# Attention and channel mix on one core: two 64-key score blocks merged into 64 columns before the softmax

## The chip, the cores and the metric

The kernel runs on one core of a Trainium2 chip. The metric is device time in microseconds (us). The engines are PE (TensorE, matrix products and transposes), DVE (VectorE), ACT (ScalarE), POOL (GpSimd) and SP (SyncE, which here issues all DMAs). Every engine runs its own list of instructions strictly in order; semaphores hold an instruction until what it reads has been made. SBUF is the on-chip memory that all engines read, PSUM the accumulator memory that PE writes (8 banks of 128 partitions x 512 float32).

## The reference

Window attention, then a channel mix in the manner of RWKV, all in float32 (the weights arrive as float64, eight bytes each):

```
q, k, v: (8 batches, 8 heads, 576, 64)            # window 64
scores = (q @ k^T) / 8;  key j counts for query i if 0 <= i - j < 64, else -1e9
attn   = exp(scores - rowmax);  attn /= (rowsum + 1e-9);  x = attn @ v     -> (8, 576, 512)
x_prev = x shifted by one position, zero at the start of each batch
xk = mu_k * x + (1 - mu_k) * x_prev               # mu_r the same for xr
xr = mu_r * x + (1 - mu_r) * x_prev
k  = relu(xk @ w_k)          # w_k 512 x 1024
v  = (k * k) @ w_v           # w_v 1024 x 512
r  = sigmoid(xr @ w_r)       # w_r 512 x 512
out = r * v
```

A query sees at most 64 keys. Cut into blocks of 64 positions, query row r of a block sees keys r+1 to 63 of the block before and keys 0 to r of its own.

## The kernel before

**Attention.** The 8 x 9 blocks of 64 queries are taken for two heads at a time (a head pair fills 128 partitions). A group holds up to 8 such halves; there are 37 groups. For each group PE makes the scores, 128 key columns for each query, in two PSUM banks `s` (one for each head of the pair). DVE runs 8 fused instructions (scale, add the mask, negate, running minimum) over 128 columns each, from `s` to the SBUF tile `pr`; ACT makes 8 exponentials with row sums; DVE adds the epsilon and takes reciprocals (`rs`); POOL scales 8 pieces of `pr` by `rs`; PE transposes them in two blocks of four (`t`, one bank); ACT copies the two banks to `pt`; PE multiplies by the values (`x`, 128 keys deep, one bank) and ACT copies the result to `xT`, one row of 576 positions for each channel chunk and batch.

**Mix.** The 72 blocks are then taken in 11 units of 4, 5 and nine times 7 blocks, so 256, 320 or 448 columns. For each unit and each of 4 channel chunks, `d = x - x_prev` is made and blended with mu, once for xk and once for xr (in the first two units ACT makes mu-scaled x_prev instead of the difference). Each float32 operand of the products is split into a high and a low part, and every product is three matmul passes; a unit has 240 matmuls into the PSUM banks `m`, of which there are four. ACT makes the high parts, POOL or DVE the low ones.

**Weights.** 20 chunks of 128 x 512 float64 (4 of w_r, 8 of w_k, 8 of w_v) are loaded and turned into float32 by bit operations: ACT takes an absolute value, DVE clamps (in SBUF), shifts into a PSUM bank `wp` (one of the `m` banks), merges the sign and exponent there and merges the low word back into SBUF (`wt`); ACT and POOL then split high and low (`ws`).

**What sets the order.** All this is written as pieces with an engine, a key, a cost, needs and the buffers that they take. `play()` steps through time: on each engine that is free it starts the piece with the lowest key whose needs are done (plus a lag) and whose buffers are free. The engines' lists in the compiled program follow that order. An initial load gets a lag from a running count of bytes (`bus`); a load with a key (a prefetch of a later group) gets a fixed lag. `BEGIN` gives the keys of the attention groups, `DECODE` those of the weight chunks; the mix of unit u has keys from 40 u. In the profile the helper's line (74 before) stands for nearly all instructions, so tiles are told apart by name.

The pieces that the change touches are `soften` (softmax of a group), `scores` and `values`, `keep_x`, `decode`, `mix`, `transfer` and the loads.

Of the kernel before, what the change touches and what calls it, by code (L numbers as in the profile page):

```python
# [14 lines left out]
ALU = mybir.AluOpType  # L15
PSUM = bass.MemoryType.PSUM
# [7 lines left out]
G = 4  # L24
UNITS = (4, 5) + (7,) * 9
TU = max(UNITS) * W
# [3 lines left out]
FAR = 3.0e38  # L30
# [3 lines left out]
XB = 9  # L34
TB = 5
# [9 lines left out]
EARLY = 7  # L45
# [7 lines left out]
def attn_rwkv_kernel(ctx, tc, qT, kT, v2, mu_k, mu_r, w_k, w_v, w_r, out):  # L53
# [6 lines left out]
    ps_s = ctx.enter_context(tc.tile_pool(name="ps_s", bufs=2, space=PSUM))  # L60
    ps_t = ctx.enter_context(tc.tile_pool(name="ps_t", bufs=1, space=PSUM))
    ps_x = ctx.enter_context(tc.tile_pool(name="ps_x", bufs=1, space=PSUM))
    ps_m = ctx.enter_context(tc.tile_pool(name="ps_m", bufs=4, space=PSUM))


    class Engine:
# [5 lines left out]
        def __getattr__(self, name):  # L72
# [4 lines left out]
    room = {"tmp": TB, "m": 4, "s": 2, "t": 1, "x": 1, "pr": 3, "sums": 4, "pt": 2, "xT": XB,  # L77
            "ks": 8, "r": R_BUFS, "xr": 1, "xk": 1, "qk": 2, "v": 3}
# [59 lines left out]
    def over(n):  # L138

        return 75 + 1.15 * n  # L140


# [5 lines left out]
    masks = {}  # L148
    for first in (None, 0, 1):
        masks[first] = const.tile([P, P], F32, name=f"mask{first}")  # L150
        nc.gpsimd.memset(masks[first], 0.0)
        for j in range(2):
            m = masks[first][j * W:(j + 1) * W]
            if j == first:
                nc.gpsimd.affine_select(out=m, in_=m, compare_op=ALU.is_ge, fill=NEG, base=0,
                                        pattern=[[-1, P]], channel_multiplier=1)
                continue
            nc.gpsimd.affine_select(out=m, in_=m, compare_op=ALU.is_ge, fill=NEG, base=-1,
                                    pattern=[[1, P]], channel_multiplier=-1)
            nc.gpsimd.affine_select(out=m, in_=m, compare_op=ALU.is_ge, fill=NEG, base=W,  # L160
                                    pattern=[[-1, P]], channel_multiplier=1)
# [5 lines left out]

# [19 lines left out]

    words = {}

    def decode(n, loaded):
        ws, _, i, c = chunks[n]
        key = DECODE[n]
        word, bits = Hold("tmp"), Hold("m")
# [5 lines left out]
        def clamp():  # L202
# [8 lines left out]
        def top():  # L211
            dve.scalar_tensor_tensor(words[n, 0], raw[n][:, :, 1], 0xC0000000, words[n, 0],
                                     op0=ALU.bitwise_and, op1=ALU.bitwise_or)

        def low():
            dve.scalar_tensor_tensor(words[n].bitcast(U32), raw[n][:, :, 0], 29, words[n, 0],
                                     op0=ALU.logical_shift_right, op1=ALU.bitwise_or)
# [8 lines left out]
        p = Piece("ACT", key, 680, sign, [loaded], takes=[word])  # L226
        p = Piece("DVE", key, 440, clamp, [p])
        p = Piece("DVE", key, 725, shift, [p], takes=[bits])
        p = Piece("DVE", key, 725, top, [p])
        p = Piece("DVE", key, 725, low, [p], uses=[bits])  # L230
        p0 = Piece("ACT", key, 630, first_part, [p])
# [14 lines left out]
    def load_qk(n, i0=0, i1=NB, key=None):  # L246

        takes = []
        if i0 == 0:
            held[n] = [Hold("xT"), Hold("xT")] if n in (2, 3) else [Hold("qk")]  # L250
            takes = held[n]

        def load():
            if i0 == 0:
                places(n)
            q, k = loaded[n]
            dma.dma_start(k[:, i0 * W:i1 * W], kT[n, :, i0 * W:i1 * W])
            dma.dma_start(q[:, i0 * W:i1 * W], qT[n, :, i0 * W:i1 * W])

        p = transfer(load, 2 * 4 * P * W * (i1 - i0), takes, key=key)  # L260
        arrived.update(((n, i), p) for i in range(i0, i1))

    def places(n):

        if n in (2, 3):
            loaded[n] = [act.tile([P, 1 + S], F32, name=nm, tag="xT", bufs=XB)[:, :S] for nm in "qk"]
        else:
            loaded[n] = [ld.tile([P, S], F32, name=nm) for nm in "qk"]

    def load_v(n, c0=0, c1=4, d0=0, d1=4, key=None):  # L270

        takes = []
        if c0 == 0:
            held["v", n] = [Hold("ks"), Hold("ks")] if n == 3 else [Hold("v")]
            takes = held["v", n]

        def load():
            if c0 == 0:
                if n == 3:
                    v = [act.tile([P, 4, P], F32, name="vs", tag="ks", bufs=8) for _ in range(2)]  # L280
                else:
                    v = ld.tile([P, 2, 4, P], F32, name="v", bufs=3)
                    v = [v[:, 0], v[:, 1]]
                loaded["v", n] = v
            v = loaded["v", n]
            dma.dma_start(v[0][:, c0:c1], v2[n, :, 0, c0:c1])
            dma.dma_start(v[1][:, d0:d1], v2[n, :, 1, d0:d1])

        p = transfer(load, 4 * P * P * (c1 - c0 + d1 - d0), takes, key=key)
        arrived.update(((n, 0, c), p) for c in range(c0, c1))  # L290
        arrived.update(((n, 1, c), p) for c in range(d0, d1))


    def slot(*blocks):
        return list(zip(blocks[::2], blocks[1::2]))

    groups = [slot(*((n, i) for n in (n0, n0 + 1) for i in range(i0, i0 + 4)))
              for i0 in (0, 4) for n0 in (0, 2)] + [slot(*((n, NB - 1) for n in range(NP)))]
    blocks = [(n, i) for n in range(NP, B * NP) for i in range(NB)]
    groups += [slot(*blocks[o:o + 2 * G]) for o in range(0, len(blocks), 2 * G)]  # L300

    first = {n: min(t for t, sl in enumerate(groups) for s in sl for m, _ in s if m == n)
             for n in range(B * NP)}
    banks, weights, sums, flipped = {}, {}, {}, {}
    xTs, got = {}, {}
    chain = {}

    def new_xT():

        xT = act.tile([P, 1 + S], F32, name="xT", tag="xT", bufs=XB)  # L310
        dve.memset(xT[:, 0:1], 0.0)
        return xT

    def chunk(i):
        return (0, i // 2) if (i % 2 or i == 0) else (1, i // 2 - 1)

    def scores(t):

        banks[t] = [ps_s.tile([P, G, P], F32, name="s") for _ in range(2)]
        for e, halves in enumerate(groups[t]):  # L320
            for j, (n, i) in enumerate(halves):
                q, k = loaded[n]
                k0 = max(i - 1, 0) * W
                for h in range(2):
                    hr = slice(h * W, (h + 1) * W)
                    pe.matmul(banks[t][h][j * W:(j + 1) * W, e, :], q[hr, i * W:(i + 1) * W],
                              k[hr, k0:k0 + P], start=True, stop=True)

    def values(t):
        ps = flipped[t] = ps_x.tile([P, 2 * G, W], F32, name="x")  # L330
        for o, (n, i, e, j) in enumerate(order(t)):
            a, c = chunk(i)
            for h in range(2):
                pe.matmul(ps[h * W:(h + 1) * W, o, :], loaded["v", n][a][:, c, h * W:(h + 1) * W],
                          flipped[t, h][:, e, j * W:(j + 1) * W], start=True, stop=True)

    def order(t):
        return sorted((n, i, e, j) for e, halves in enumerate(groups[t]) for j, (n, i) in enumerate(halves))

    def burst(t, ts, tv):  # L340

        needs, takes, uses, cost = [], [], [], 400
        if ts is not None:
            for n, i in (half for halves in groups[ts] for half in halves):
# [362 lines left out]
```

## Time and profile before

| What | Value |
|---|---|
| Median of 3 runs | 677.83 us (677.21 to 679.62) |
| Span of the profiled execution | 676.3 us |
| PE busy | 641.3 us (95%) |
| DVE busy | 422.9 us (63%) |
| ACT busy | 373.1 us (55%) |
| POOL busy | 346.8 us (51%) |
| Moved by DMA | 56.50 MB, 84 GB/s over the span |

The profile is one execution and has no time of its own beside the span; the median of the runs lies 1.5 us above it. Busy times of PE are modelled from pipelined starts, so a row's mean is the latency of one matmul, and starts that follow each other give its cost. A row of the timeline is: start, length, engine, line, operation, output<-input tiles, shape, count. The mean busy share hides that the program has two stages, a start in which weights come in and are decoded, and a long stretch in which they stay in SBUF.

### The profile page before, as it was taken

The numbers are of one execution on the slowest core, as the hardware profiler recorded it, in microseconds if no ns is written. First come the engines' busy times: TensorE is split into PE (matmuls) and PEld (weight loads), VectorE is DVE, ScalarE is ACT, GpSimd is POOL, SyncE is SP. The second block draws the span as 40 slices with busy tenths as digits, with TensorE's granted clock in tenths as the row PEclk, the third lists the DMA queues.
The fourth block names the chain that finished last, engine by engine and source line by source line (L and its number), as shares of the span: only waits on it lengthen the run. The fifth ranks groups of instructions, "written<-read, shape, count | busy, mean of one in ns | idle before, by whom it ended". The sixth has DMA issues, their size and how long they took to land.

```text
span 676.3 us, 14360 instructions
## 1 busy us (share of the span) xinstructions
PE 641.3 (95%) x5232; PEld 575.0 (85%) x5232; DVE 422.9 (63%) x1358; ACT 373.1 (55%) x1127; POOL 346.8 (51%) x503
## 2 busy tenths in 40 slices
PE   4749799999999999999999999999999999999997
PEld 3538689998888888888898789888888888999997
DVE  5899964844882696367648615952794397276241
ACT  6878777656763765665465526535654662242330
POOL 5756785584455555455554625454563465244310
PEclk9868899999999999999999999999999999999999
DMA  8971324222321224312212202232213000001001
GB/s 258 329 301 61 105 75 127 78 97 67 109 83 63 68 70 143 108 67 81 74 36 68 95 28 67 67 108 80 67 64 122 6 1 28 29 1 38 17 1 55
DMA packets 33766, 56.50 MB, mean 84 GB/s; under 512 B 5024, under 2 KB 16800, under 8 KB 33696
## 3 DMA queue, kind: packets, MB, share of 16 engines
q1 hardware_dynamic: 33696, 55.59, 24.3%
q8 instruction: 41, 0.67, 0.4%
q14 instruction: 29, 0.24, 0.1%
HBM read 46.14 MB, written 9.44 MB: 82 GB/s over the span
## 4 chain that ended last, share of the span: by engine, by line
PE 79%; DVE 9%; POOL 5%; issue 3%; ACT 2%; DMA 1%; SPq 0%; POOLq 0%; ACTq 0%
PE m L74 64%; PE x L74 5%; PE s L74 5%; PE t L74 4%; DVE d L74 3%; POOL pr L74 3%; DVE r L74 2%; DVE ks L74 1%; POOL ws L74 1%; DMA q<-qT 1%; DVE pr L74 1%; DVE wt L74 1%; DVE wp L74 1%; DVE th L74 1%; ACT pr L74 1%
## 5 line engine op out<-in xcount | busy, mean ns | idle before, releaser
L74 PE MATMUL m<-xk,ws 128*128 128x448 f32 (+2 forms) x1056 | 221.1, 359 | 0.0
L74 PE MATMUL m<-ks,ws 128*128 128x448 f32 (+2 forms) x1056 | 218.1, 356 | 2.2 <-DVE ks L74 2.2
L74 PEld LDWEIGHTS m<-ks,ws 128*128 128x128 f32 x1056 | 186.6, 188 | 16.3 <-DVE ks L74 2.6
L74 PEld LDWEIGHTS m<-xk,ws 128*128 128x128 f32 x1056 | 188.2, 191 | 13.6
L74 POOL TENSOR_SCALAR pr<-pr,rs 128x128 f32<-128x128 f32 x288 | 133.7, 482 | 114.2 <-DVE rs L74 97.7
L74 DVE TENSOR_TENSOR ks<-kf,ks 128x448 fp32r<-128x448 f32 (+2 forms) x88 | 60.7, 702 | 123.1 <-ACT ks L74 122.5
L74 POOL TENSOR_TENSOR kf<-kf 128x448 f32<-128x448 f32 (+2 forms) x88 | 79.3, 905 | 108.8 <-ACT kf L74 108.4
L74 PE MATMUL m<-xr,ws 128*128 128x448 f32 (+2 forms) x528 | 113.3, 359 | 8.3 <-ACT r L74 5.6
L74 ACT ACTIVATE pr<-pr,nmax 128x128 f32<-128x128 f32 x288 | 111.9, 393 | 10.7 <-DVE nmax L74 8.1
L74 PEld LDWEIGHTS m<-xr,ws 128*128 128x128 f32 x528 | 94.6, 191 | 16.3 <-ACT r L74 5.8
L74 ACT COPY pt<-t 128x512 f32<-128x512 f32 (+1 forms) x74 | 42.4, 574 | 74.3 <-PE t L74 74.1
L74 POOL TENSOR_TENSOR xk<-d,xk 128x448 fp32r<-128x448 f32 (+2 forms) x44 | 55.3, 1263 | 39.4 <-ACT xk L74 39.4
L74 DVE TENSOR_TENSOR d<-xT 128x448 f32<-128x448 f32 (+6 forms) x120 | 72.1, 604 | 0.2
L74 ACT ACTIVATE kf<-m 128x448 f32<-128x448 f32 (+2 forms) x88 | 44.8, 516 | 45.3 <-PE m L74 42.2
L74 PE MATMUL t<-ident,pr 128*128 128x128 f32 x288 | 51.9, 289 | 13.7 <-POOL pr L74 11.1
L74 ACT CAST ks<-kf 128x448 fp32r<-128x448 f32 (+2 forms) x88 | 46.4, 543 | 29.6 <-POOL kf L74 29.6
L74 POOL TENSOR_TENSOR xr<-d,xr 128x448 fp32r<-128x448 f32 (+2 forms) x44 | 50.6, 1164 | 22.7 <-ACT xr L74 22.7
L74 DVE CUSTOM_DVE_ANT_0 pr<-s,maskNone 128x128 f32<-128x128 f32 x224 | 53.8, 285 | 12.1 <-PE s L74 12.0
L74 DVE SCALAR_TENSOR_TENSOR r<-m,r 128x448 f32<-128x448 f32 (+2 forms) x44 | 25.8, 591 | 55.3 <-PE m L74 55.3
L74 PEld LDWEIGHTS t<-ident,pr 128*128 128x128 f32 x288 | 37.2, 144 | 26.6 <-POOL pr L74 20.2
L74 ACT ACTIVATION_READ_ACCUMULATOR pr<-pr,nmax 128x1 f32 x288 | 54.9, 191 | 0.0
L74 PE MATMUL s<-k,q 64*64 64x128 f32 x1152 | 44.5, 294 | 7.0 <-DMA q<-qT 6.9
(46 smaller groups left out, 578.8 us busy)
## 6 DMA issues: line engine op xcount, KB each, us to landing
v<-v SPq DMA_DIRECT2D x56, 256.0 KB, 4.1
k<-kT SPq DMA_DIRECT2D x28, 288.0 KB, 2.8
q<-qT SPq DMA_DIRECT2D x28, 288.0 KB, 3.3
w<-w_k SPq DMA_DIRECT2D x8, 512.0 KB, 6.3
w<-w_v SPq DMA_DIRECT2D x8, 512.0 KB, 10.2
outT<-r SPq DMA_DIRECT2D x12, 224.0 KB, 1.9
w<-w_r SPq DMA_DIRECT2D x4, 512.0 KB, 4.5
outT<-r SPq DMA_DIRECT2D x12, 160.0 KB, 1.8
```

The lines of the kernel that those rows point to most:

```text
L74: return lambda *args, **kw: tc.keep_in_program_order(op(*args, **kw))
```

## The change

One change in many places:

- **Groups** are now 36 pairs of blocks with all 8 heads each. Each group loads its own q (128 x 4 x 128), k (128 x 4 x 192) and v (six tiles of 64 rows, one for each half of the partitions and each of three blocks).
- **Scores** are the same matmuls, into one tile `s` of two banks. `pack` then merges the two key blocks: where a mask `own` (key column not after the query row) is set, a predicated copy puts the score of the query's own block over that of the block before, in PSUM; 512 columns remain for 8 heads x 2 blocks. A reduction takes the maximum, one subtraction writes `pr`.
- **Softmax** on those 512 columns: one exponential on ACT, `shares` (a sum, the epsilon, a reciprocal) on DVE, one multiplication by the reciprocals on POOL.
- **Transposes**: four for each group (144 in all, 288 before). `keep` copies the bank twice, on DVE, each time multiplied by a mask of one side (`sides`), into `pt`.
- **Values**: 64 matmuls of 64 keys x 64 columns for each group, own block and previous block accumulated, into two banks `x`.
- **x** lies in `xu`, one tile for each unit with all 4 chunks. In `mix` the difference `d` is made once and used for xk and xr.
- **Decode** is in place in SBUF: the four DVE instructions are one piece and take no PSUM bank.
- PSUM: `s` one tile of two banks, `t` one, `x` two, `m` three. The `spare` rule goes, costs and `BEGIN` are new, the fixed lag of a keyed load is 2600 instead of 2000.

```diff
-BEGIN = (-30, -29, 0, 6, 12, 18, 26, 34, 43, *range(53, 184, 10),
+BEGIN = (-30, -28, 2, 14, 24, 34, 43, *range(53, 184, 10),
          196, 210, 223, 236, 250, 263, 277, 286, 295, 304, 312, 322, 332, 342, 352)
...
-    room = {"tmp": TB, "m": 4, "s": 2, "t": 1, "x": 1, "pr": 3, "sums": 4, "pt": 2, "xT": XB,
-            "ks": 8, "r": R_BUFS, "xr": 1, "xk": 1, "qk": 2, "v": 3}
+    room = {"tmp": TB, "m": 3, "s": 1, "t": 1, "x": 1, "pr": 2, "sums": 4, "pt": 2, "xu": 2,
+            "ks": 8, "r": R_BUFS, "xr": 1, "xk": 1, "q": 2, "k": 2, "v": 3}
...
-        def shift():
-            words[n, 0] = ps_m.tile([P, WC], U32, name="wp", tag="m")
-            dve.tensor_scalar(words[n, 0], words[n].bitcast(U32), 3, 0x3FFFFFF8,
-                              op0=ALU.logical_shift_left, op1=ALU.bitwise_and)
...
+        def bits():
+            word = words[n].bitcast(U32)
+            dve.tensor_scalar(words[n], words[n], HI_MIN, HI_MAX, op0=ALU.max, op1=ALU.min)
+            dve.tensor_scalar(word, word, 3, 0x3FFFFFF8, op0=ALU.logical_shift_left, op1=ALU.bitwise_and)
+            dve.scalar_tensor_tensor(word, raw[n][:, :, 1], 0xC0000000, word, op0=ALU.bitwise_and, op1=ALU.bitwise_or)
+            dve.scalar_tensor_tensor(word, raw[n][:, :, 0], 29, word, op0=ALU.logical_shift_right, op1=ALU.bitwise_or)
...
-        p = Piece("SP", len(pieces) - 9999 if key is None else key, 60, fn, needs, takes, lag=2000)
+        p = Piece("SP", len(pieces) - 9999 if key is None else key, 60, fn, needs, takes, lag=2600)
...
+        def pack():
+            s8 = s4.rearrange("q h e k -> q (h e) k")
+            if block(g, 0)[1] and block(g, 1)[1]:
+                dve.copy_predicated(s8[:, :, :W], wide(own.bitcast(U32), 8), s8[:, :, W:])
...
+            dve.tensor_reduce(sums[g][0], s8[:, :, :W], axis=AX.X, op=ALU.max)
+            dve.tensor_sub(weights[g], s8[:, :, :W], sums[g][0].unsqueeze(2).to_broadcast([P, 8, W]))
+        def exp():
+            sca.activation(weights[g], weights[g], AF.Exp, scale=SCALE)
+        def shares():
+            dve.tensor_reduce(total, weights[g], axis=AX.X, op=ALU.add)
+            dve.tensor_scalar_add(rs, total, EPS)
+            dve.reciprocal(rs, rs)
+        def scale():
+            pool.tensor_mul(weights[g], weights[g], sums[g][2].unsqueeze(2).to_broadcast([P, 8, W]))
+        def flip():
+            for e in range(4):
+                pe.transpose(ps[:, e], weights[g][:, 2 * e:2 * e + 2].rearrange("q e k -> q (e k)"), ident)
+        def keep():
+            for a in (1, 0):
+                dve.tensor_mul(sided[g][:, a].rearrange("q e (j r) -> q (e j) r", j=2),
+                               flipped[g].rearrange("q e (j r) -> q (e j) r", j=2), wide(sides[:, a], 8))
...
+    def prefetch(t):
+        for what, g in (("q", t + 2), ("k", t + 2), ("v", t + 2)):
+            if 2 <= g < GROUPS:
+                load(what, g, key=BEGIN[t])
...
+    load("q", 0)
+    load("k", 0)
+    load_w(2)
+    load("v", 0)
+    load("q", 1)
+    load("k", 1)
+    load_w(2)
+    load("v", 1)
+    load_w(len(chunks) - len(raw))
```

The order of instructions changes most at the start. On SP, before, the first rows are the loads of q and k of the first head pairs among the first weight chunks (`q_128`, `k_129` and so on are those of one head pair):

```order
L74 DMA w_126<-w_r 128x1024
L74 DMA k_129<-kT 128x256
L74 DMA q_128<-qT 128x256
L74 DMA k_133<-kT 128x256
L74 DMA q_132<-qT 128x256
L74 DMA w_136<-w_r 128x1024
L74 DMA k_139<-kT 128x256
L74 DMA q_138<-qT 128x256
L74 DMA k_143<-kT 128x256 [waits DMAHW0_49]
```

In the changed kernel SP holds at these places (`q_108`, `k_112` and `q_123`, `k_125` belong to groups 0 and 1, `q_196`, `k_208` to group 2):

```order
L71 DMA q_108<-qT 128x4x128
L71 DMA k_112<-kT 128x4x128
...
L71 DMA q_123<-qT 128x4x128 [waits DMAHW0_49]
L71 DMA k_125<-kT 128x4x192 [waits DMAHW1_49]
...
L71 DMA w_168<-w_v 128x1024 [waits DMAHW2_49]
L71 DMA w_170<-w_v 128x1024 [waits DMAHW3_49]
...
L71 DMA q_196<-qT 128x4x128 [waits DMAHW2_49,PE_49]
L71 DMA k_208<-kT 128x4x192 [waits DMAHW3_49]
```

The eight semaphores DMAHW0 to DMAHW7 are taken in turn, so `q_196` is issued once the transfer of `w_168` has landed, and `k_208` once that of `w_170`, the last weight chunk, has. Both stood nowhere near this place before: no load of the first four groups was behind the last weight chunks.

On PE, before, two groups of scores come first, then transposes and values of the first group:

```order
L74 MATMUL s<-k,q 64x128 [waits DMAHW2_49,DMAHW1_49]
L74 MATMUL s<-k,q 64x128 x7
L74 MATMUL s<-k,q 64x128 [waits DMAHW4_49,DMAHW3_49]
L74 MATMUL s<-k,q 64x128 x7
L74 MATMUL s<-k,q 64x128 [waits DMAHW6_49,DMAHW7_49,DVE_49,PE_49]
L74 MATMUL s<-k,q 64x128 [waits DVE_49,PE_49]
L74 MATMUL s<-k,q 64x128 x6
L74 MATMUL s<-k,q 64x128 [waits DMAHW1_49,DMAHW0_49]
L74 MATMUL s<-k,q 64x128 x7
L74 MATMUL t<-ident,pr 128x128 [waits Pool_49] x4
```

Now (`s_179` is group 0, `s_219` group 2, `s_274` group 1, `t_262` and `x_300` group 0):

```order
L71 MATMUL s_179<-k_112,q_108 64x64 [waits DMAHW1_49,DMAHW0_49]
L71 MATMUL s_179<-k_112,q_108 64x64 x7
L71 MATMUL s_179<-k_112,q_108 64x128 x8
L71 MATMUL s_219<-k_208,q_196 64x128 [waits DMAHW2_49,DMAHW3_49,DVE_49,PE_49]
L71 MATMUL s_219<-k_208,q_196 64x128 x15
L71 MATMUL t_262<-ident_82,pr_198 128x128 [waits Pool_49]
L71 MATMUL t_262<-ident_82,pr_198 128x128 x3
L71 MATMUL s_274<-k_125,q_123 64x128 [waits DMAHW0_49,DMAHW1_49,DVE_49,PE_49]
L71 MATMUL s_274<-k_125,q_123 64x128 x15
L71 MATMUL x_300<-pt_270,v_118 64x64 [waits DMAHW4_49,DVE_49]
```

The scores of group 2 now stand as the second burst of all, ahead of the transposes of group 0 and the scores of group 1.

DVE follows with the decode chunks behind that burst's first reader. Before, its list begins with the first chunk and the maxima of group 0:

```order
L74 TENSOR_SCALAR wt<-wt 128x512 [waits Activation_49]
L74 TENSOR_SCALAR wp<-wt 128x512 [waits DVE_49]
L74 SCALAR_TENSOR_TENSOR wp<-w,wp 128x512 [waits DMAHW0_49,DVE_49]
L74 SCALAR_TENSOR_TENSOR wt<-w,wp 128x512 [waits DVE_49]
L74 ISA pr,nmax<-s,mask_101 128x128 [waits PE_49,Pool_49]
```

Now, after the pack of group 0, two chunks and the mu vectors (`wt_268` is the third chunk):

```order
L71 TENSOR_SCALAR mu1_107<-muk_105 128x4 [waits DMAHW2_49]
L71 TENSOR_SCALAR mu1_107<-mur_106 128x4 [waits DMAHW3_49]
L71 COPY_PREDICATED s_219<-own_87,s_219 128x8x64 [waits PE_49]
L71 TENSOR_REDUCE most_256<-s_219 128x8 [waits DVE_49]
L71 TENSOR_TENSOR pr_255<-s_219,most_256 128x512 [waits DVE_49]
L71 TENSOR_TENSOR pt_270<-t_262,sides_89 128x512 [waits PE_49,Pool_49]
L71 TENSOR_TENSOR pt_270<-t_262,sides_89 128x512
L71 TENSOR_SCALAR wt_268<-wt_268 128x512 [waits Activation_49]
```

The predicated copy of `s_219` reads the scores of group 2. The decode of `wt_268`, the third chunk, and of the seventeen after it stand behind that row in DVE's list.

More of the change, by code (lines that the diff above doesn't have):

```diff
@@ L224, in second_part @@
             pool.tensor_sub(ws[i, c][:, 1], words[n], ws[i, c][:, 0].bitcast(F32))
[L226 to L231, printed above, removed]
+        p = Piece("ACT", key, 600, sign, [loaded], takes=[word])
+        p = Piece("DVE", key, 2000, bits, [p])
+        p0 = Piece("ACT", key, 540, first_part, [p])
         decoded[id(ws), i, c] = p0, Piece("POOL", key, 1280, second_part, [p0], uses=[word])
@@ L329, in values @@
[L329 to L338, printed above, removed]
@@ new lines, in block, with scores @@
+    def block(g, s):
+        return divmod(2 * g + s, NB)
+    banks, weights, sums, flipped, sided, crossed = {}, {}, {}, {}, {}, {}
+    xs_of, got, opened_x = {}, {}, {}
+    chain = {}
+    def scores(g):
+        banks[g] = ps_s.tile([P, 2, 4, P], F32, name="s")
+        q, k = loaded["q", g], loaded["k", g]
+        for s in range(2):
+            o = 0 if block(g, s)[1] else W
+            for p in range(2):
+                for h in range(2):
+                    for j in range(2):
+                        hr, n = slice(h * W, (h + 1) * W), 2 * j + p
+                        pe.matmul(banks[g][j * W:(j + 1) * W, h, 2 * s + p, o:], q[hr, n, s * W:(s + 1) * W],
+                                  k[hr, n, s * W + o:(s + 2) * W], start=True, stop=True)
@@ L356, in burst @@
+    def burst(key, gs, gv):
+        needs, takes, uses, cost = [], [], [], 100
+        if gs is not None:
+            needs += [arrived["q", gs], arrived["k", gs]]
+            uses += [held["q", gs], held["k", gs]]
+            takes.append(Hold("s"))
+            cost += 900
+        if gv is not None:
             bank = Hold("x")
+            needs += [arrived["v", gv], chain["kept", gv]]
+            uses += [held["v", gv], chain["pt", gv]]
             takes.append(bank)
+            cost += 1050
@@ L359, in fn @@
         def fn():
-            if ts is not None:
-                scores(ts)
-            if tv is not None:
-                values(tv)
-        p = Piece("PE", BEGIN[t] if t < len(BEGIN) else BEGIN[-1] + 9, cost, fn, needs, takes, set(uses), lag=200)
-        if tv is not None:
-            runs = []
-            for o, (n, i, _, _) in enumerate(order(tv)):
-                if runs and runs[-1][0] == n and runs[-1][2] == i - 1:
-                    runs[-1][2] = i
-                else:
-                    runs.append([n, i, i, o])
-            for run in runs:
-                keep_x(p, tv, bank, *run)
@@ new lines, in fn @@
+            if gs is not None:
+                scores(gs)
+            if gv is not None:
+                values(gv)
+        p = Piece("PE", key, cost, fn, needs, takes, uses, lag=200)
+        if gv is not None:
+            units = [max(u for u in range(len(UNITS)) if FIRST[u] <= 2 * gv + s) for s in range(2)]
+            if units[0] == units[1] and block(gv, 1)[1]:
+                keep_x(p, gv, bank, units[0], 0, 2)
+            else:
+                keep_x(p, gv, bank, units[0], 0, 1)
+                keep_x(p, gv, bank, units[1], 1, 1)
@@ L442, in keep @@
-            sca.copy(flipped[t, h][:, :count], ps[:, :count])
-        bank, kept = Hold("t"), Hold("pt")
-        q = Piece("PE", key + 1, 110 * count, flip, scaled, [bank], [rows], lag=200)
-        q = Piece("ACT", key + 1, over(P * count), keep, [q], [kept], [bank])
-        chain.setdefault((t, "kept"), []).append(q)
-        chain.setdefault((t, "pt"), []).append(kept)
-    def prefetch(t):
-        for n in range(NP, B * NP):
-            if first[n] == t + 1:
-                load_qk(n, key=BEGIN[t])
-            if first[n] == t:
-                load_v(n, key=BEGIN[t])
@@ new lines, in soften @@
+        tbank, kept = Hold("t"), Hold("pt")
+        q = Piece("DVE", key + 0.5, 2000, pack, [p], [rows, sm], [bank], lag=120)
+        q = Piece("ACT", key + 0.5, 530, exp, [q], lag=120)
+        q = Piece("DVE", key + 0.5, 1000, shares, [q], lag=120)
+        q = Piece("POOL", key + 0.5, 1300, scale, [q], uses=[sm])
+        q = Piece("PE", key + 1, 530, flip, [q], [tbank], [rows], lag=200)
+        chain["kept", g] = Piece("DVE", key + 1, 1250, keep, [q], [kept], [tbank])
+        chain["pt", g] = kept
@@ L509, in mix, with low @@
-        return p, Piece("POOL", key, 160 + 2.35 * o, low, [p], uses=[scratch])
+                sca.copy(xs[0][:, 0, c, :n], e[0][:, :n])
+            def low(e=e, xs=xs):
+                pool.tensor_sub(xs[0][:, 1, c, :n], e[0][:, :n], xs[0][:, 0, c, :n].bitcast(F32))
+            if u >= 2:
+                p = Piece("DVE", key, over(n), blend, [pk], [own_], [held["x", u], scratch])
+            else:
+                p = Piece("ACT", key, acts(n) + 60, before,
+                          {got[t] for t in range(FIRST[u], FIRST[u + 1])} | {arrived["mu"], mixing.get(u)},
+                          [own_] + ([hold] if c == 0 else []))
+                mixing[u] = p
+                p = Piece("DVE", key, over(n), blend, [p], uses=[held["x", u]])
```

421 lines of the change are left out of this document (182 added, 239 removed).

## The prediction

> **What bounds the kernel now.** I read the page's busy shares and its chain first, then busy time by stretch, then what PE waits for in the first 100 us.
>
> ```profile
> span 676.3 us, 14360 instructions
> PE 641.3 (95%) x5232; PEld 575.0 (85%) x5232; DVE 422.9 (63%) x1358; ACT 373.1 (55%) x1127; POOL 346.8 (51%) x503
> PE 79%; DVE 9%; POOL 5%; issue 3%; ACT 2%; DMA 1%; SPq 0%; POOLq 0%; ACTq 0%
> ```
>
> PE ends last. The stretches (time, then busy time of PE, PEld, DVE, ACT, POOL, then granted clock, DMA share, GB/s) show that this is two kernels in one:
>
> ```profile
> 0.00:25.00 25.00, 14.89 (x166) 11.39 (x170) 14.82 (x64) 17.84 (x56) 14.40 (x40) 0.95 0.86 281
> 25.00:50.00 25.00, 12.54 (x83) 10.43 (x75) 24.61 (x60) 18.52 (x49) 17.23 (x21) 0.77 0.86 320
> 50.00:75.00 25.00, 22.52 (x248) 18.87 (x248) 24.28 (x74) 19.10 (x58) 17.60 (x26) 0.80 0.16 49
> 150.00:350.00 200.00, 200.00 (x1771) 178.69 (x1770) 123.76 (x463) 118.82 (x380) 105.49 (x165) 1.00 0.25 82
> ```
>
> From 25 to 75 us DVE is busy 98% of the time and PE half idle: the decode of the weights bounds. From 150 us on PE never stops, and DVE is at 62%. So an edit is worth PE's own time in the long stretch and DVE's time, or what DVE waits for, in the start. The start ends with the last decode instruction on DVE (84.49) and the first product of unit 1 (93.96), from where PE keeps running:
>
> ```profile
> 84.49 0.69 DVE L74 SCALAR_TENSOR_TENSOR wt<-w,wp 128x512 uint32<-128x512 uint32 x1
> 93.96 0.60 PE L74 MATMUL m<-xk,ws 128*128 128x320 f32 x3
> ```
>
> **The long stretch.** One group in PE's timeline:
>
> ```profile
> 167.32 1.10 PE L74 MATMUL s<-k,q 64*64 64x128 f32 x32
> 168.36 1.15 PE L74 MATMUL x<-pt,v 128*64 128x64 f32 x32
> 169.44 0.88 PE L74 MATMUL m<-xk,ws 128*128 128x448 f32 x3
> ...
> 171.39 5.07 PE L74 MATMUL m<-xr,ws 128*128 128x448 f32 x24
> 176.29 0.60 PE L74 MATMUL t<-ident,pr 128*128 128x128 f32 x4
> 176.65 2.71 PE L74 MATMUL m<-xr,ws 128*128 128x448 f32 x12
> 179.19 0.60 PE L74 MATMUL t<-ident,pr 128*128 128x128 f32 x4
> 179.55 0.86 PE L74 MATMUL m<-xr,ws 128*128 128x448 f32 x3
> 577.12 18.16 PE L74 MATMUL m<-xk,ws 128*128 128x448 f32 x90
> ```
>
> The last row gives about 0.2 us for an `m` matmul (18.16 less one matmul's latency, over 90). Between 171.39 and 179.55 stand 36 of them, 7.2 us, and two blocks of four transposes: 8.16 - 7.2 = 0.95, so some 0.47 us a block. One block of two goes in each group: about 30 groups lie behind the start, -14 us. Scores keep their 1.04 us (start to start, 167.32 to 168.36). Values had 32 matmuls of 128 keys by 64 columns in 1.08 us. Now they are 64 of 64 by 64, four places of the array side by side as for the scores, so 64 x 64 / 4 = 1024 columns in a row, as many as 32 x 128 / 4 in the scores: the same 1.05 us. Saved with that is the change of shape between the two bursts (0.04 to 0.1 us each, 30 times, some 2 us). Together -16; a burst that the start leaves over takes back 1, so **-15 us**.
>
> That holds if the columns set a burst's time and not the number of instructions. At half clock the same bursts read:
>
> ```profile
> 51.13 1.99 PE L74 MATMUL s<-k,q 64*64 64x128 f32 x32
> 53.05 1.97 PE L74 MATMUL x<-pt,v 128*64 128x64 f32 x32
> 54.95 2.31 PE L74 MATMUL m<-xk,ws 128*128 128x256 f32 x11
> ```
>
> 1.92 and 1.90 us, nearly double, so the array sets them; what 64 instructions would take if issue set them, no row shows: between 1.05 and twice 1.08. I take 1.05.
>
> The other engines stay behind PE. ACT loses 8 exponentials and a bank copy for each group, POOL 7 of 8 scalings. DVE takes on about 2 us more for each group of some 14 us, and loses half of the differences: it comes to about three quarters. A fourth `m` bank less leaves three products of 12 x 0.2 us ahead of an eviction of half a microsecond. I cost these at nothing; PE's products cover them.
>
> **The start: who waits for group 2.** Here the new order decides. PE's second burst is now the scores of group 2, whose k is issued only when the last weight chunk has landed. PE runs in order, so the transposes of group 0, the scores of group 1 and all products stand behind it; DVE runs in order, so the pack of group 2 holds back 18 of the 20 chunks. ACT, POOL and SP run dry behind these two. When does it land? By the shapes 13.4 MB have to come before it (20 chunks of 0.52 MB, three groups of about 1 MB). The transfers before:
>
> ```profile
> GB/s 0 229 354 301 219 341 398 310 133 325 235 235 359 389 405 222 335 357 358 309 268 325 380 369 415 421 418 429 410 426 303 27 0 0 0 0 0 0 0 0
> DMA packets 7781, 15.01 MB, mean 250 GB/s; under 512 B 1120, under 2 KB 5216, under 8 KB 7776
> ```
>
> (40 slices of 1.5 us.) 15 MB ended at about 46.5 us; the last 1.6 MB took 4, so 13.4 MB were there at 42.6. Fewer of the bytes are in small packets now, with weights alone at some 420 GB/s as in the late slices it would be 38. I take 40; the bounds are 37 and 45. The scores then end at 42, the pack of group 2 at about 44. Before, the same queue had the first four groups in front of the weights, and DVE was at work all that time; now it has done two packs' worth and two chunks by 16 us and stands for about 26.
>
> From 44 on DVE has to do 18 chunks and what stands between them. Prices:
>
> ```profile
> L74 DVE TENSOR_SCALAR wt<-wt 128x512 f32<-128x512 f32 x20 | 10.0, 502 | 5.5 <-ACT wt L74 5.4
> L74 DVE TENSOR_SCALAR wp<-wt 128x512 uint32<-128x512 uint32 x20 | 13.6, 685 | 0.1
> L74 DVE SCALAR_TENSOR_TENSOR wt<-w,wp 128x512 uint32<-128x512 uint32 x20 | 13.4, 675 | 0.1
> L74 DVE SCALAR_TENSOR_TENSOR r<-th,r x4: 424/900/1466, 46.5 to 57.9; 128x256 f32<-128x256 f32 x4
> L74 DVE TENSOR_TENSOR ks<-kf,ks x7: 406/426/1490, 60.4 to 87.8; 128x256 fp32r<-128x256 f32 x7
> L74 DVE SCALAR_TENSOR_TENSOR d<-xT,muk,d x4: 473/762/1158, 23.9 to 30.8; 128x256 f32<-128x256 f32 x4
> ```
>
> A chunk is two one-input and two two-input instructions of 512 columns. In SBUF the shift will cost like the clamp (0.42 undisturbed, 0.50 in the mean), so about 2 x 0.45 + 2 x 0.7 = 2.35: 18 x 2.35 = 42.5. Each 512-column step of the softmax at 0.69: two packs of three, 4.2; three `shares`, 3.2 with their two short steps; three `keep` of two, 3.9. The rest at the least values of the last three rows: 8 blends 3.8, four gates of r with two one-input steps each 4.0, 6 ks 2.5. Sum 64, from 44 to 108, if nothing else is in the way.
>
> **A port that DVE and POOL share.** It is in the way. Min, median and max above differ by a microsecond for one shape, and the timeline shows when:
>
> ```profile
> 76.47 2.71 POOL L74 TENSOR_TENSOR ws<-wt,ws 128x512 fp32r<-128x512 f32 x2 [2.23 <-ACT ws L74]
> 77.97 1.49 DVE L74 TENSOR_TENSOR ks<-kf,ks 128x256 fp32r<-128x256 f32 x1
> 79.38 0.68 DVE L74 TENSOR_SCALAR wp<-wt 128x512 uint32<-128x512 uint32 x1
> ```
>
> A DVE instruction with both inputs in SBUF that meets a POOL subtraction ends just behind it, 1.05 us late. Before, the decode kept an operand in PSUM and was spared: the excess over the least values is 6.8 us (4 x 0.5 in r, 7 x 0.38 in ks, 8 x 0.27 in the blends). Now all four decode instructions are in SBUF and POOL's scaling has two tensor inputs. Bounds: 6.5 as before, and 23 if each of 18 subtractions and 4 scalings costs 1.05. I take 14, the middle: **the last decode ends at 122**.
>
> In the Trainium skill, "SBUF — State Buffer", section "SBUF: two separate sides", the port pair that VectorE and GpSimd share is an exclusive lock: the loser blocks for the whole instruction. The rows above agree; read strictly it speaks for the upper bound.
>
> Behind the last decode stand two ks (0.8), pack of group 4 (2.1), exponential (0.6), `shares` (1.05), scaling (1.3), transposes (0.5), `keep` (1.3), values (1.1), copies (0.9) and the first mix of unit 1 (2.5), with handoffs some 13: the first product of unit 1 at **135**, where it was at 94. So +41.
>
> **Sum.** 676.3 + 41 - 15 = 702 us of span; the median of the runs stood 1.5 above it: **703**.
>
> **Rivals.** (1) *The start stalls, the port costs little more than before.* The decode's last instruction at 114 or less, 108 at the least: median 689 to 696. For it: many POOL instructions fall into gaps of DVE. Against it: DVE has no gaps there. (2) *Issue bounds the values burst.* At 33 ns for each of 64 instructions (1.08/32) the burst takes 2.1 us, +1 in 31 groups, 31 us in all, 734 on top of the stall; half of it gives 719. The half-clock rows speak against it. The Trainium skill ("TensorE: Matmul & The Clock Gate", section "Wait — 56ns, not 53.3ns?") has a floor of about 25 ns from start to start; estimated by it the burst is 1.6 us, which is that half case. (3) *The other side: the stall is not there.* If group 2's q and k land by 16 us, when DVE comes to its pack, all the 26 us of standing go, and the decode ends near 96: 677, no change; with the port at 6.5 or less and the softmax steps of the start cheaper, 669. It decides at 16 us of landing, and each microsecond later costs one. For it: the transfer is only 0.65 MB, and a chunk's packets may leave room; against it: k is not even issued before the last weight chunk has landed.
>
> **How the numbers follow.** A measurement can tell about 0.5% (3.4 us) from no change. Forecast 0.62; rival 1 0.14; rival 2 0.06; rival 3 0.18 with its mixtures, of which 0.08 lands below 674 and 0.10 within the band. So slower 0.82, same 0.10, faster 0.08. Low end: no port cost beyond before's, loads 4 us early and a little of handoffs less, 685. High end: port at 23 (712) and loads 5 us late: 717. Rival 3 and the full rival 2 stay outside.
>
> **What would show it.** Right: PE's second `s` burst starts at 38 to 45 us, idle before it for some 30 us with a DMA of k as releaser; DVE idle from about 16; `wt` instructions of two inputs with means well above 0.7 and the `ws` ones above 1.32 us; the last `wt` near 122; from about 140 on PE without waits and 16 us less for the same work; `x` bursts of 1.05 us. Wrong: a second `s` burst before 20 us, `x` bursts near 2 us, or waits of PE for DVE in the long stretch.

## The result and the profile after

The changed kernel takes 757.1 us (median of 4 runs, 755.56 to 758.66) where the kernel before takes 678.51 beside it: a ratio of 1.115, interval 1.1115 to 1.1185. It is slower, as forecast, but by 79 us and not by 25; 757 lies far outside the range of 685 to 717. The page of the profiled execution:

```profile
span 757.0 us, 14856 instructions
PE 626.3 (83%) x6112; PEld 568.5 (75%) x6112; DVE 481.3 (64%) x854; ACT 252.5 (33%) x498; POOL 264.5 (35%) x257
PE 48%; DVE 39%; DMA 4%; ACT 3%; issue 2%; POOL 2%; SPq 1%; POOLq 0%; ACTq 0%; DVEq 0%
```

PE is busy 15 us less and yet ends 81 us later, and 39% of the chain is now DVE's, where 9% was. The first product of unit 1 divides the span in two parts that can be compared. It starts here:

```profile
143.91 0.64 PE L71 MATMUL m<-xk,ws 128*128 128x320 f32 x1 [3.58 <-ACT xk L71]
```

Busy time by stretch (columns as in the prediction), first of the kernel before, cut at its own first product of unit 1:

```profile
0.00:94.00 94.00, 65.74 (x651) 54.42 (x652) 80.37 (x253) 72.19 (x220) 63.75 (x107) 0.87 0.57 197
94.00:676.30 582.30, 575.60 (x4584) 520.60 (x4582) 342.51 (x1106) 300.93 (x908) 283.09 (x397) 1.00 0.20 65
```

and of the changed kernel:

```profile
0.00:144.00 144.00, 56.19 (x741) 50.35 (x741) 103.29 (x168) 48.43 (x100) 49.92 (x61) 0.84 0.43 132
144.00:757.00 613.00, 570.07 (x5372) 518.20 (x5372) 378.00 (x687) 204.07 (x399) 214.62 (x197) 0.96 0.22 63
```

The start is 50 us longer (forecast: 41). The long stretch is 31 us longer, where 15 less were forecast: most of what was not foreseen lies here.

**The start** went as described, a little later. The timelines of PE and of DVE:

```profile
4.57 1.56 PE L71 MATMUL s<-k,q 64*64 64x64 f32 x32 [4.57 <-DMA k<-kT]
44.10 1.98 PE L71 MATMUL s<-k,q 64*64 64x128 f32 x32 [37.97 <-DMA k<-kT]
```

```profile
46.14 0.70 DVE L71 COPY_PREDICATED s<-own,s 128x512 f32<-128x512 uint32 x1 [29.48 <-PE s L71]
129.41 1.42 DVE L71 SCALAR_TENSOR_TENSOR wt<-w,wt 128x512 uint32<-128x512 uint32 x2
```

PE waits 38 us for the k of group 2, DVE stands 29.5 us for the scores behind it, and the last decode instruction ends at 130.8 (forecast 122). From the end of that pack (48.3) it is 82.5 us, where 64 + 14 were reckoned. The chain of releases (start, length) shows why k came at 44 and not at 40:

```profile
29.96 10.62 DMA w<-w_v
40.60 3.37 DMA k<-kT
```

The last weight chunk had landed at 40.6. Only then was k issued, and its own 3.4 us up to its landing came on top.

**In the long stretch PE waits again**, mostly for one thing (total, times, longest wait; first the kernel before from 100 us on, then the changed kernel from 150 us on):

```profile
PE t L74 <- POOL pr L74: 1.7, 4, 0.5
PE t L71 <- POOL pr L71: 33.0, 12, 6.9
PE m L71 <- DVE r L71: 4.5, 3, 2.5
```

In 12 of 30 groups PE comes to the transposes before POOL has scaled that group's weights. One such place, on PE, DVE and POOL:

```profile
246.63 0.90 PE L71 MATMUL s<-k,q 64*64 64x128 f32 x32
247.35 1.11 PE L71 MATMUL x<-pt,v 64*64 64x64 f32 x64
248.39 5.73 PE L71 MATMUL m<-ks,ws 128*128 128x448 f32 x27
259.12 1.12 PE L71 MATMUL t<-ident,pr 128*128 128x128 f32 x4 [5.01 <-POOL pr L71]
259.89 2.44 PE L71 MATMUL m<-ks,ws 128*128 128x448 f32 x6
```

```profile
248.17 1.72 DVE L71 SCALAR_TENSOR_TENSOR e<-d,mur,xu 128x128 f32<-128x128 f32 x2
249.81 0.69 DVE L71 TENSOR_TENSOR d<-xu 128x128 f32<-128x128 f32 x2
250.42 1.71 DVE L71 SCALAR_TENSOR_TENSOR e<-d,muk,xu 128x128 f32<-128x128 f32 x2
...
253.31 0.61 DVE L71 COPY_PREDICATED s<-own,s 128x128 f32<-128x128 uint32 x2
...
257.65 0.20 DVE L71 RECIPROCAL rs<-rs 128x8 f32<-128x8 f32 x1
```

```profile
258.03 1.04 POOL L71 TENSOR_TENSOR pr<-pr,rs 128x512 f32<-128x512 f32 x1 [2.98 <-DVE rs L71]
```

The scores are done at 247.5. DVE is still on the mix of the next unit, so the pack begins at 253.3, and the chain of pack, exponential, sum, reciprocal and scaling ends at 259.1. PE's list has the values burst of another group and 27 product matmuls in between, which end at 254.1, and then the transposes. So PE has 6.6 us of other work behind the scores. The chain itself takes 5.8 us and would fit; it is too late because it starts 5.8 us after the scores. At the longest wait (6.9 us, up to 641.87) the pack starts 9.1 us after the scores. PE stands 5 us here, and afterwards it runs at half clock: the six products from 259.89 take 2.3 us up to the next row, 1.2 at full clock. The granted clock of these stretches:

```profile
248.00:254.00 6.00, 6.00 (x59) 5.31 (x51) 5.93 (x13) 2.51 (x5) 3.56 (x4) 1.00 0.12 41
254.00:259.00 5.00, 0.12 (x1) 0.00 (x0) 2.99 (x7) 0.63 (x1) 2.02 (x2) 0.96 0.80 230
259.00:262.00 3.00, 2.88 (x10) 2.67 (x11) 1.72 (x3) 0.00 (x0) 0.07 (x1) 0.50 0.16 43
```

### The profile page after: what moved, and what is told of

Same layout as the page of the kernel before. It is cut to its first block, busy times and chain, and to the rows that moved or that the text cites. A ratio compares the mean times of both kernels' runs of the same rounds, so it can differ in the third digit from the quotient of the medians.

```text
span 757.0 us, 14856 instructions
## 1 busy us (share of the span) xinstructions
PE 626.3 (83%) x6112; PEld 568.5 (75%) x6112; DVE 481.3 (64%) x854; ACT 252.5 (33%) x498; POOL 264.5 (35%) x257
## 4 chain that ended last, share of the span: by engine, by line
PE 48%; DVE 39%; DMA 4%; ACT 3%; issue 2%; POOL 2%; SPq 1%; POOLq 0%; ACTq 0%; DVEq 0%
PE m L71 42%; DVE e L71 11%; DVE wt L71 8%; DVE d L71 4%; DVE r L71 4%; PE s L71 2%; DVE s L71 2%; DVE pt L71 2%; PE t L71 2%; DVE most L71 2%; DVE sums L71 2%; DVE pr L71 2%; PE x L71 2%; DVE rs L71 2%; POOL pr L71 2%
## 5 line engine op out<-in xcount | busy, mean ns | idle before, releaser
L71 PEld LDWEIGHTS m<-xr,ws 128*128 128x128 f32 x528 | 96.3, 195 | 22.4 <-ACT xr L71 10.4
L71 POOL TENSOR_TENSOR xk<-e,xk 128x448 fp32r<-128x448 f32 (+2 forms) x44 | 57.5, 1306 | 117.1 <-ACT xk L71 117.1
L71 PE MATMUL s<-k,q 64*64 64x128 f32 (+1 forms) x1152 | 40.3, 280 | 43.8 <-DMA k<-kT 42.5
L71 ACT CAST ks<-kf 128x448 fp32r<-128x448 f32 (+2 forms) x88 | 47.6, 542 | 85.9 <-POOL kf L71 80.4
L71 PEld LDWEIGHTS s<-k,q 64*64 64x64 f32 x1152 | 31.8, 140 | 53.9 <-issue 49.1
L71 DVE TENSOR_TENSOR pt<-t,sides 128x512 f32<-128x512 f32 x72 | 46.2, 683 | 32.8 <-PE t L71 32.8
L71 POOL TENSOR_TENSOR pr<-pr,rs 128x512 f32<-128x512 f32 x36 | 41.5, 1154 | 65.4 <-DVE rs L71 60.1
L71 PE MATMUL t<-ident,pr 128*128 128x128 f32 x144 | 26.3, 313 | 41.2 <-POOL pr L71 41.1
L71 POOL TENSOR_TENSOR xr<-e,xr 128x448 fp32r<-128x448 f32 (+2 forms) x44 | 54.6, 1241 | 12.6 <-ACT xr L71 12.6
L71 POOL TENSOR_TENSOR ws<-wt,ws 128x512 fp32r<-128x512 f32 x20 | 27.2, 1361 | 74.4 <-ACT ws L71 65.7
L71 DVE SCALAR_TENSOR_TENSOR e<-d,muk,xu 128x448 f32<-128x448 f32 (+6 forms) x60 | 47.9, 829 | 0.6
L71 DVE COPY_PREDICATED s<-own,s 128x512 f32<-128x512 uint32 (+1 forms) x44 | 24.0, 545 | 36.1 <-PE s L71 35.7
```

What stands on the lines that cost most here:

```text
L71: return lambda *args, **kw: tc.keep_in_program_order(op(*args, **kw))
```

## The experiments

Each kernel was timed beside the kernel before on one chip; three chips were used in all, so the ratios are what can be compared. Four theories were tried: that the start is lost to the load of group 2; that the long stretch is lost to too little room in PE's list between a group's scores and its transposes; that decoding in SBUF costs DVE time; and that DVE's total work, not the order, is the trouble (the rival of all three).

### The arrival of group 2

The changed kernel with one condition: the first keyed loads get their arrival from the count of bytes.

```diff
-        if key is None:
+        if key is None or key == BEGIN[0]:
             bus[0] = max(bus[0], 1300) + size / 300
             p.lag = bus[0] + 900
```

> The changed kernel with one line different: the planner gives the loads of group 2 an arrival from its count of bytes, as it does for the initial loads, instead of a flat 2.6 us. The same instructions; PE's second burst of scores is then that of group 1. Theory A (the start is lost to PE and DVE standing for group 2's k, 29.5 us on DVE): first product of unit 1 falls from 143.9 to 110-120 us, time 725-735 us (757 less 25 to 32). Theory B (the loads and the decode fill the start anyway, the standing is hidden): first product of unit 1 after 135 us, time 748 us or more.

735.17 us (ratio to the kernel before 1.084, 1.0809 to 1.0871). The planner now puts group 1's scores second, and the first product of unit 1 comes at 120.7:

```profile
120.72 0.64 PE L71 MATMUL m<-xk,ws 128*128 128x320 f32 x1 [3.59 <-ACT xk L71]
```

22 us less, a little under the range of theory A: the 29.5 us of standing are gone, but not all of them come back, since DVE is then 97% busy from 25 to 100 us. So 23 of the 50 us by which the start is longer are the place of this one load in the order; the rest lies elsewhere.

### The room between scores and transposes

The changed kernel, planner costs only:

```diff
-        q = Piece("DVE", key + 0.5, 2000, pack, [p], [rows, sm], [bank], lag=120)
-        q = Piece("ACT", key + 0.5, 530, exp, [q], lag=120)
+        slow = 1.6 if key >= 48 else 1.0
+        q = Piece("DVE", key + 0.5, 2000 * slow, pack, [p], [rows, sm], [bank], lag=120)
+        q = Piece("ACT", key + 0.5, 530 * slow, exp, [q], lag=120)
...          # shares 1000, scale 1300 and keep 1250 likewise
```

> The changed kernel with the planner's costs of the softmax pieces (pack, exp, shares, scale, keep) 1.6 times as large from the seventh group on. The same instructions; PE's list has 42 to 48 product matmuls between a group's scores and its transposes where the changed kernel has 27 to 30. Theory A (in the long stretch PE waits for the scaled scores because the list leaves only 28 x 0.2 = 5.6 us for a chain of at least 5.5 us that the mix on DVE delays): waits of PE for POOL pr fall from 30 to under 10 us, time 720-735 us. Theory B (DVE has too much work, wherever the transposes stand): the waits move to other tiles, time 748 us or more.

717.19 us (1.0569, 1.0544 to 1.0594): 40 us less with the same instructions, 3 us below the range of theory A. (The factor sets in with group 7, counted from 0.) What PE waits for from 150 us on:

```profile
PE m L71 <- DVE r L71: 3.4, 4, 2.5
PE x L71 <- DVE pt L71: 2.4, 1, 2.4
PE t L71 <- POOL pr L71: 1.5, 3, 0.7
```

33.0 us of waiting for `pr` became 1.5, and little took its place (2.4 us for `pt`). The long stretch fell from 613 to 572 us:

```profile
144.00:715.90 571.90, 558.38 (x5372) 509.64 (x5372) 373.84 (x687) 203.93 (x400) 209.94 (x197) 0.99 0.24 67
```

Of the 41 us, 29 are idle time of PE and 12 are busy time, at a mean clock of 0.99 in place of 0.96. DVE does as much work there as it did (374 us against 378), so it was not overloaded; the transposes stood too early. That it is their place that counts, and not an earlier start of the softmax, one group shows:

```profile
296.86 1.10 PE L71 MATMUL s<-k,q 64*64 64x128 f32 x32
297.78 1.11 PE L71 MATMUL x<-pt,v 64*64 64x64 f32 x64
298.82 6.94 PE L71 MATMUL m<-ks,ws 128*128 128x448 f32 x33
305.95 3.31 PE L71 MATMUL m<-ks,ws 128*128 128x448 f32 x15 [0.19 <-DVE r L71]
309.96 0.66 PE L71 MATMUL t<-ident,pr 128*128 128x128 f32 x4 [0.71 <-POOL pr L71]
```

Here too the mix is ahead on DVE: the pack starts at 303.23, 5.3 us after the scores, and the scaling ends at 309.90, 11.9 us after them (11.5 at the place above). With 48 products in between PE waits 0.7 us in place of 5.0.

The mirror of it on the kernel before, whose planner costs grow from group 7 on:

```diff
-EARLY = 7
+EARLY = 99
```

> The kernel before with the planner's costs of maximum, exponential and scaling kept at their small values (215, 390, 365) for all groups, where they grow to 375, 590 and 500 from the seventh group on. The same instructions; PE's list has 24 to 30 product matmuls between a group's scores and its last transpose where before it has 33 to 39. Theory A (the margin in the list is what keeps PE from waiting): PE waits for POOL pr in the long stretch rise from 3 to 15 us or more, time 690 us or more. Theory B (the margin matters only because the changed kernel's DVE chain is longer; here the pieces are small and ready): under 682 us.

709.77 us (1.0447, 1.0413 to 1.0481): 32 us lost by three planner costs and no change of an instruction. (The expectation's counts, 24 to 30 and 33 to 39 products, are those up to a group's first transposes; up to its last there are 30 to 42 here in most groups, 42 to 54 before.) 17.1 us are named waits, where the kernel before has 1.7:

```profile
PE t L74 <- POOL pr L74: 17.1, 36, 1.7
```

```profile
200.60 0.33 PE L74 MATMUL t<-ident,pr 128*128 128x128 f32 x1 [0.42 <-POOL pr L74]
201.39 0.33 PE L74 MATMUL t<-ident,pr 128*128 128x128 f32 x1 [0.46 <-POOL pr L74]
```

The rest stands in PE's busy time (658.48 us in all against 641.34). Transposes that come one by one show 0.33 us each there, instead of some 0.12 in a block of four, and the mean clock from 100 us on is 0.99 instead of 1.00; how the 17 us divide between the two was not separated. The kernel before had the same weakness, kept covered by the larger costs.

### Decode in SBUF, alone

The kernel before, with the shift and the merge written into the SBUF tile. The planner still takes the bank, so all lists keep their order:

```diff
-            words[n, 0] = ps_m.tile([P, WC], U32, name="wp", tag="m")
+            words[n, 0] = words[n].bitcast(U32)
```

> The kernel before with one part of the change alone: the shift and merge of the decode write the SBUF tile instead of a PSUM bank; the bank is still taken by the planner, so every engine's list stays in the same order. Theory A (DVE and POOL block each other when both work in SBUF): two-input wt instructions from 0.68 to about 0.95 us in the mean, clamp from 0.50 to 0.63, shift 0.69 as before; a chunk +0.7 us, 20 chunks +14 us of DVE work in a start that DVE bounds, time 687-694 us. Theory B (what DVE loses falls into its gaps): 677-681 us.

691.38 us (1.0193, 1.0178 to 1.0208), 13 us more. The groups of decode instructions up to 120 us:

```profile
L74 DVE SCALAR_TENSOR_TENSOR wt<-w,wt 128x512 uint32<-128x512 uint32 x40 | 33.5, 847 | 0.1
L74 DVE TENSOR_SCALAR wt<-wt 128x512 uint32<-128x512 uint32 x20 | 11.5, 579 | 0.1
L74 DVE TENSOR_SCALAR wt<-wt 128x512 f32<-128x512 f32 x20 | 10.9, 549 | 5.1 <-ACT wt L74 5.0
```

The two-input instructions take 0.85 in place of 0.68 us, less than expected, and the last decode ends 10 us later (95.2 against 85.2), the first product of unit 1 12 us later (106.1). In SBUF the shift takes 0.42 us in the median against 0.69; that gain is more than lost. The time is that of theory A, its sum is not: the decode instructions cost DVE 5.3 us more (55.9 against 50.6) and not 14. Up to the last decode DVE is busy 5.6 us longer and idle 4.4 us longer. POOL pays too: its scalings of 128 columns up to 120 us take 0.58 us in the mean where they took 0.45. So the loss lies on both engines, which fits a port where either waits for the other.

### Sum of the two planner edits, and the decode back in PSUM

Both planner edits together:

> The changed kernel with both edits of the planner, the arrival of group 2 and the 1.6-fold costs of the softmax pieces. Theory A (two separate losses, one in the start and one in the long stretch): they add, 757 - 22 - 40 = 695 us, 691-699; first product of unit 1 near 121 us, waits of PE for POOL pr after 150 us under 10 us. Theory B (both delays overlap, the list that is later at the start has the waits anyway): 705-717 us.

694.08 us (1.0218, 1.0183 to 1.0253). 757 - 22 - 40 = 695: the two losses add, as theory A has it.

Then the decode through one of the three `m` banks, with the old rule that products of unit 0 leave one free, and with a planner cost of 2500 instead of 2000 for its DVE piece:

```diff
-            dve.tensor_scalar(word, word, 3, 0x3FFFFFF8, ...)
+            wp = ps_m.tile([P, WC], U32, name="wp", tag="m")
+            dve.tensor_scalar(wp, word, 3, 0x3FFFFFF8, ...)
...          # both merges read wp, the first writes it; the piece takes Hold("m")
-            ps, bank, p = product(key, wr_s, ..., NC, n)
+            ps, bank, p = product(key, wr_s, ..., NC, n, spare=key < USTEPS)
```

> The kernel with both planner edits, and the decode again through a PSUM bank of the three m banks (with the rule of the kernel before that products of unit 0 leave one bank free); the decode pieces stand later and more spread on DVE for that. Theory A (the rest of the start's loss is the port that DVE and POOL share): a chunk falls from 3.3 to 2.5-2.6 us on DVE, two-input instructions to 0.68, first product of unit 1 from 121 to 104-110 us, time 679-687 us. Theory B (the start is then bound by the softmax steps on DVE or by banks): first product of unit 1 stays above 115 us, time 689 us or more.

682.14 us (1.0049, 1.0034 to 1.0065), first product of unit 1 at 108.9 instead of 120.7. A chunk is 2.85 us on DVE (3.35 in SBUF, in the run before it), more than the 2.5 to 2.6 expected, because the clamp still works in SBUF:

```profile
L71 DVE TENSOR_SCALAR wt<-wt 128x512 f32<-128x512 f32 x20 | 15.4, 769 | 0.0
L71 DVE SCALAR_TENSOR_TENSOR wp<-w,wp 128x512 uint32<-128x512 uint32 x20 | 13.9, 696 | 0.7
```

Each of the three PSUM steps is at its undisturbed 0.69 (no single one took over 0.70); the clamp, 0.42 undisturbed, is at 0.77 in the mean and 1.51 at most. By these means the decode accounts for 20 x 0.50 = 10 of the 11.8 us; what the rule, the cost and the new order did beside it was not separated.

The same with 1.8-fold costs:

> As the one with the decode in PSUM, with 1.8-fold instead of 1.6-fold planner costs of the softmax from the seventh group on: 48 to 51 product matmuls between scores and transposes, 45 there. Theory A (what is left of PE's waits in the long stretch, 8 us with 1.6-fold, is still margin): 4 to 8 us less than with 1.6-fold. Theory B (what is left comes from the mix or from gated outputs): within 2 us of it.

680.47 us (1.0025, 1.0009 to 1.0041). The profile's long stretch is 4.3 us shorter than with 1.6, but the medians differ by 1.7 only: by time theory B, by place A. Its long stretch:

```profile
110.00:677.20 567.20, 554.57 (x5372) 506.74 (x5372) 375.69 (x688) 203.56 (x399) 210.23 (x197) 1.00 0.24 68
```

567.2 us against 582.3 before: -15.1, the number of the prediction. It is made up otherwise than forecast. PE's busy time is 21.0 us less (554.6 against 575.6), some 3 of them because 20 products of unit 0 lie behind the cut in the kernel before, and PE's idle time is 5.9 us more. This execution was also 1.6 us faster than the kernel's median.

### Trying to shorten the start further

The clamp of all chunks on POOL, in the last kernel and in the kernel before:

```diff
-            dve.tensor_scalar(words[n], words[n], HI_MIN, HI_MAX, op0=ALU.max, op1=ALU.min)
+            pool.tensor_scalar(words[n], words[n], HI_MIN, HI_MAX, op0=ALU.max, op1=ALU.min)
```

> As the one with the decode in PSUM and 1.8-fold costs, and the clamp of each weight chunk on POOL instead of DVE (0.77 us each there, 15.4 us in all, of which 7 is waiting for POOL). The three decode instructions left on DVE all have an operand in PSUM. Theory A (DVE's work still bounds the start): last decode on DVE from 94.7 to 80-87, first product of unit 1 from 110 to 96-103, time 667-674 us. Theory B (POOL, with 20 more instructions of some 1.2 us, or the chain of group 4 bounds it): first product of unit 1 above 107, time 677 us or more.

> The kernel before with only the clamp of the decode moved from DVE to POOL. Theory A (DVE bounds the start there as well, 98% busy from 25 to 75 us): 10 us less on DVE, time 666-673 us. Theory B (POOL's added work, 20 instructions beside 8 scalings for each group, takes the gain back): 676-682 us.

684.32 us (1.0094, 1.0074 to 1.0114) and 694.78 us (1.0247, 1.0228 to 1.0267): worse both times, the second by 13 us more than theory B allowed. POOL is busy 95% of the time from 25 to 75 us in both. The clamp is slow there (the group of the kernel before with its clamp on POOL):

```profile
L74 POOL TENSOR_SCALAR wt<-wt 128x512 f32<-128x512 f32 x20 | 38.4, 1926 | 3.2 <-ACT wt L74 2.7
```

and among the waits of DVE in that kernel stand 22.4 us for it:

```profile
DVE wp L74 <- POOL wt L74: 22.4, 15, 7.3
```

In the changed one DVE's named waits for it are only 1.5 us; its last decode ends at 91.3 instead of 94.7, and yet the first product of unit 1 comes at 112.0 instead of 110.0. Both lists were planned with 1000 ns for a clamp that takes 1930, so part of the loss may be a list that is too tight again; that was not tested on these two.

A third of the clamps on POOL (`if n % 3 == 2`), planned at 1930 ns:

> As the one with the decode in PSUM and 1.8-fold costs, with the clamp of every third weight chunk (6 of 20) on POOL, where a clamp of all chunks on POOL took 1.94 us each and filled POOL to 97% from 25 to 75 us. Theory A (DVE bounds the start as long as POOL has room): 6 x 0.77 = 4.6 us less on DVE, POOL at some 75%, first product of unit 1 near 105, time 674-678 us. Theory B (a clamp on POOL holds the shared port for its 1.9 us and gives the gain back): 679-683 us.

678.6 us beside 678.75 for the kernel before (0.9998, 0.9979 to 1.0018): no difference from it, and 1.8 us less than without by the ratios. The time lies between the two ranges. By place theory A fails: the first product of unit 1 moves only from 110.0 to 108.8 and the last decode not at all (94.7), though DVE has 6 clamps less. Whether the port takes the gain back, as theory B says, is not shown.

And the mix three keys earlier on top of it:

```diff
-            keys = [base - 40 + k for k in (25, 29, 33, 37)]
+            keys = [base - 40 + k for k in (22, 26, 30, 34)]
```

> As the one with every third clamp on POOL, and the mix of each unit from the third on with keys lower by 3, so that DVE takes it up some 3 us earlier. PE's waits on the first products of units 2 and 3 (for the mix, 9 us in all with 1.8-fold costs) should go. Theory A (these waits are the mix being late): 3 to 8 us less than the one with every third clamp. Theory B (an earlier mix only delays the softmax): within 2 us of it or slower.

681.7 us (1.0035, 1.0014 to 1.0056), 3 us slower: PE's waits for `r` went from 4.4 to 5.6 us, those for the mix (`xk`) fell from 5.5 to 4.6 only. That is theory B. No version beat the kernel before; the best equals it.

## Why the prediction was wrong

- **The sign and the place of the stall were right.** PE's second `s` burst started at 44.1 (forecast 38 to 45) after 38 us of waiting for the k of group 2, and DVE stood from 16.6 to 46.1. Undoing it alone gave 22 us.
- **The start was mis-sized by 9 us.** The k of group 2 came 4 us later than the 40 I took (45 was my bound): the bytes ahead of it were there at 40.6, but I had no term for its own transfer of 3.4 us behind them. And DVE needed 82.5 us where 78 were reckoned. The port term was near: 16 us by the decode's own means (3.26 us a chunk against 2.35, 18 chunks) where 14 were taken for everything. The handoffs behind the last decode took 13.1 us, as forecast. The decode back in PSUM moved the first product of unit 1 by 11.8 us, and the decode in SBUF alone cost the kernel before 13 us. The Trainium skill's lock ("SBUF — State Buffer", section "SBUF: two separate sides") agrees with this: the steps with an operand in PSUM stood at 0.69 us beside a busy POOL, while in SBUF the two-input steps rose from 0.69 to 0.96 and the clamp from 0.42 to 0.63 in the mean.
- **The step that failed is "The other engines stay behind PE. ... I cost these at nothing; PE's products cover them."** I compared busy shares and took slack in the mean for cover at each place. The share was even lower than I reckoned: 62% of the long stretch (378 of 613 us) where I had three quarters, and PE waited all the same. What covers a group's softmax is only what stands in PE's own list between its scores and its transposes: the values burst and 27 to 36 products for most groups of the changed order from 200 us on, where the kernel before mostly has 33 to 42 ahead of a group's first transposes and 42 to 54 ahead of its last. I did not count. With 27 products it is 6.6 us, while the chain is 5.8 us when DVE takes it up at once (253.31 to 259.07) and 11.5 us from the scores when the mix of a unit is ahead of it. So most groups did not wait, and all five with 27 products did. It cost 33 us of waits for `pr`, and with the slower matmuls behind them 41 us of the long stretch (613 to 572); adding the margin gave 40 us of time, taking it from the kernel before cost 32. I had named "waits of PE for DVE in the long stretch" as a sign that I was wrong, without a price; the waits read POOL `pr`, and DVE stands behind them.
- **The PE term was right in kind, and its number partly by luck.** With the margin at 1.8 the long stretch is 15.1 us shorter than before, as forecast for a PE without waits; but it is the sum of 21.0 us less busy time and 5.9 us more idle time.
- **The values burst** stayed at 1.04 us (102.88 to 103.92):

```profile
102.88 1.11 PE L71 MATMUL x<-pt,v 64*64 64x64 f32 x64
103.92 4.03 PE L71 MATMUL m<-xk,ws 128*128 128x256 f32 x33
```

  64 records in 1.04 us are 16 ns each, so rival 2 falls. The floor of 25 ns from start to start that the Trainium skill names ("TensorE: Matmul & The Clock Gate", section "Wait — 56ns, not 53.3ns?"), and that I had carried over to this burst at four places of the array, does not show here; the measurement decides.
- **Rival 1** (little loss at the port) is ruled out by the decode's means, **rival 3** (no stall) by the 38 us wait.
- **The low end of my range does not follow from its terms.** 703 less 7.5 for the port and 4 for the loads is 691.5; "a little of handoffs less" does not make it 685. The result lies at the other end, so nothing hangs on it.

What remains open: with all three losses undone the start is still 15 to 16 us longer than before (109 or 110 us against 94), which the 15 us gained later just pay for. DVE is 96% busy there from 25 to 75 us, and up to the first product of unit 1 it is busy 96.1 us where it was 80.4 before, 15.7 us more, with softmax steps that ACT had before (the row sums and the copies of the transposes) and clamps that POOL delays. How the 15 us divide between these was not separated, and two attempts to take work off DVE gained 1 us there or lost 2.

## What to carry to other kernels

Where engines run their lists in order, slack is not a share of busy time: for each chain that leaves PE and comes back, count the work that stands in PE's list between the two ends and compare it with the chain at its slowest, not at its mean. Planner costs equal to undisturbed durations leave no room for anything that is late; costs that look wrong may be what keeps the list loose. And a load's assumed arrival orders every list behind it, so a flat lag for a load that queues behind ten megabytes of weights can stop every engine behind it.

## What was not expected of the hardware

- After PE stood 5 us, its granted clock was 0.50 for some 3 us, and matmuls took twice as long: a wait of 5 us cost about 6.5. Over the long stretch the mean clock was 0.96 where it had been 1.00.
- The clamp on POOL, with one tensor input, was dearer than a subtraction with two: 1.93 us for 512 columns against 1.3 for the same shape (1.29 and 1.31 in the same two runs).
- 64 matmuls of 64 x 64 x 64 at four places of the array went by in 1.04 us, 16 ns each, no longer than the 32 of 128 x 64 x 64 that they replace (1.08 us).
